# Block-diagonal probability tiles in the token stage of a memory-augmented attention kernel, one core

## The chip, the cores and the metric

The kernel runs on one core of a Trainium2 chip. The metric is the device time of one execution in microseconds (us). The core has a matrix engine (PE, with its weight loads shown apart as PEld), a vector engine (DVE), a scalar engine (ACT), a general engine (POOL) and a queue engine (SP). They run side by side, each in the order of its own instructions, and wait for each other by semaphores. SBUF is the working memory of 128 partitions, PSUM the memory that PE writes to.

## What is computed

The program computes a gated sum of two attention layers, and the gradients of all its inputs. Only the second layer, B, matters here: 2048 tokens in 64 segments of 32, 32 heads of width 128, and 8 memory rows that each segment hands to the next.

```python
for s in range(n_seg):                       # 64 segments of 32 tokens
    h = concatenate([mem, xs], axis=1)       # 8 memory rows, 32 tokens
    q, k, v = h @ Wq, h @ Wk, h @ Wv         # per head
    scores = where(mask, q @ k.T * scale, -1e9)
    p = softmax(scores)
    o = p @ v
    o = o @ Wo
    mem = o[:M]
    outs.append(o[M:])
...
_out, _vjp = jax.vjp(_f, ...)
_grads = _vjp(grad_out)
```

Token rows attend to the 32 tokens of their own segment and to the 8 memory rows of their segment. Backward, with dP the gradient of the probabilities and dS = P * (dP - row sum) * scale, the gradient of q is dS times the keys. Both products, P times the values and dS times the keys, have a part over the 32 tokens and a part over the memory rows.

## The kernel before

The memory rows of all segments are run first, in a chain over the segments. The token rows no longer depend on each other after that, and one stage (`b_bulk`) does their forward and their backward pass. A later stage, woven with a second chain, does the backward pass of the memory rows.

`b_bulk` works on groups: 128 tokens (four segments) by four heads, 128 groups in all. Four groups make a chunk, for which inputs are loaded and outputs stored on SP's queue. The main loop runs over ticks `t`. In each tick the list `order` names 18 steps, and a step with the number `n` works on group `t - n`, so that a tick holds a step of some ten different groups. The order of the steps is the order of the instructions on every engine; nothing is rearranged by a scheduler in this stage.

The names in a tick, in the order of the list:

- `st_QT` transposes q of group t on PE into the PSUM buffer `x_tr` (two such buffers serve all transpositions in turn). `dS` of group t-8 rides along as a fifth block. DVE copies the four blocks to `x_qT` (L836), the fifth into the right half of `x_DT` (L822), and transposes the token part of `dS` in 32 by 32 blocks straight from SBUF into its left half (L823).
- `st_KT` does the same with k of group t (`x_kT`) and with `P` of group t-3 (`x_PT`).
- `st_Om` (group t-4) multiplies the memory part: the transposed memory half of `x_PT` times the values of the memory rows, which lie block-diagonally in `x_vmB`, into `x_po`.
- `st_OT` (t-5) transposes o, ACT copies it to `x_oT` (L935), and POOL multiplies it with `x_dOT` into `x_prod` (L938), from which the row sums come. `st_VT` transposes v, copied by ACT. `st_B` (four pieces spread over the tick) multiplies o by Wo into `x_b`.
- `st_SDm` and `st_SDx` compute scores and dP in one PSUM bank, `x_SD`: memory part, then token part. ACT takes the exponential into `x_E` (L891), DVE forms `x_dS` (L897).
- `st_GT` transposes dO; DVE copies it to `x_dOT` (L836).
- `st_Qm` (t-9) is the memory part of dq, into a second `x_po`. `st_K` multiplies for the gradients of the memory's k and v, in every second tick.
- `st_R` (t-2): DVE sums the rows of `x_E` (`x_l`, L911), takes the reciprocal (`x_r`, L913), and POOL multiplies both to `x_P` (L915).
- `st_M` (t-1) masks `x_E` on DVE (L904).
- `st_Ox` (t-4) and `st_Qx` (t-9) add the token parts. For each head i and each segment c a product of 32 by 32 weights with 32 by 128 values, placed on the diagonal of the PE array, sixteen in each step:

```python
self.mm(po[r32, i, :], lhsT=PT[r32, 32 * i:32 * i + 32], rhs=v[r32, i, :],
        start=False, stop=True, tp=(32 * c, 32 * c))
```

ACT copies the result out (L808) into `x_o` or `x_dq`.

DVE's order in a tick is thus: x_qT, x_DT (copy, transposition), x_kT, x_PT (copy, transposition), x_dOT, x_l, x_r, x_dS, mask. POOL's is x_prod, x_P.

Of the kernel before, what the change touches and what calls it, by code (L numbers as in the profile page):

```python
# [10 lines left out]
ALU = mybir.AluOpType  # L11
AX = mybir.AxisListType
BF16 = mybir.dt.bfloat16
# [3 lines left out]
P = 128  # L17
# [8 lines left out]
SEG = 32  # L26
# [25 lines left out]
class Kern:  # L52
# [675 lines left out]
    def b_bulk(self, wp, lp, sp, psum):  # L728
        nc = self.nc
        NTT = self.NTT  # L730
        mx = self.maskX
        mB = {w: [wp.tile([P, 4, 4, E], BF16, name=f"x_{w}mB{i}") for i in range(2)] for w in ("k", "v")}
        mT = {}
        C = {}
        NG = NTT * 8
        NC = NTT * 2

        def load(c, names):
            if c >= NC:
                return  # L740
            tt, h0 = c // 2, 16 * (c % 2)
            d = C.setdefault(c, {})
            for w in names:
                if w == "mT":
                    if c % 2 == 0:
                        mT[tt] = {}
                        for x in ("k", "v"):
                            mT[tt][x] = lp.tile([P, 4, HB, 8], BF16, name=f"x_{x}mT", bufs=2)
                            nc.sync.dma_start(mT[tt][x][:], self.mTd[x][4 * tt:4 * tt + 4].rearrange("s p h t -> p s h t"))
                elif w in ("kB", "vB"):  # L750
                    for i in range(4):
                        nc.sync.dma_start(
                            mB[w[0]][c % 2][32 * i:32 * i + 32, :, i, :],
                            self.mtok[w[0]][tt * 32:(tt + 1) * 32, h0 * P:h0 * P + 2048]
                            .rearrange("r (g i e) -> r g i e", i=4, e=E)[:, :, i, :])
                else:
                    d[w] = lp.tile([P, 16, P], BF16, name=f"x_{w}", bufs=BQ if w in deep else 3)
                    nc.sync.dma_start(d[w][:].rearrange("p h e -> p (h e)"),
                                      self.xtok[w][tt * P:(tt + 1) * P, h0 * P:h0 * P + 2048])
# [5 lines left out]
        def chunk(t, w, shape, bufs):  # L765
            d = C[t // 4]
            if w not in d:
                d[w] = sp.tile(shape, BF16, name=f"x_{w}", bufs=bufs)
            return d[w]

        def view(t):
            return t // 8, t % 8, slice(4 * (t % 4), 4 * (t % 4) + 4), C[t // 4]
# [13 lines left out]
        def flush(end=False):  # L786
            for dst, src in due.pop(0):
                (nc.scalar if end else nc.sync).dma_start(dst, src)
            due.append([])

        def transp(d, r, nm, pt):
            self.tr(pt[:, 4, :], d[:, 1, r, :].rearrange("p i t -> p (i t)"), P)
            o = sp.tile([P, 256], BF16, name=nm, bufs=2)
            return o, d[:, 0, r, :].rearrange("p i t -> p (i t)")

        def attend_m(PT, m):
            po = psum.tile([P, 4, P], F32, name="x_po", bufs=2)
            self.mm(po[:].rearrange("p i e -> p (i e)"), lhsT=PT[:, 128:256], rhs=m.rearrange("p i e -> p (i e)"),
                    start=True, stop=False)
            return po  # L800

        def attend_x(o, po, PT, v):
            for i in range(4):
                for c in range(4):
                    r32 = slice(32 * c, 32 * c + 32)
                    self.mm(po[r32, i, :], lhsT=PT[r32, 32 * i:32 * i + 32], rhs=v[r32, i, :],
                            start=False, stop=True, tp=(32 * c, 32 * c))
            nc.scalar.copy(o, po[:])  # L808

        sc = {}  # L810

        def trans(t, w, nb, ride=None):
            pt = psum.tile([P, 5, P], BF16, name="x_tr", bufs=2)
            if 0 <= t < NG:
                tt, g, r, d = view(t)
                for i in range(4):
                    self.tr(pt[:, i, :], d[w][:, 4 * (g % 4) + i, :], P)
            o2 = ride and ride(pt)
            if 0 <= t < NG:
                trans_out(t, w, nb, pt)  # L820
            if o2:
                nc.vector.tensor_copy(o2[0][:, 128:256], pt[:, 4, :])  # L822
                nc.vector.transpose(o2[0][:, 0:128], o2[1])  # L823

        def trans_out(t, w, nb, pt):
            tt, g, r, d = view(t)
            if w == "v":
                o = chunk(t, "vT", [P, 4, 16, SEG], 2)
                nc.scalar.copy(o[:, :, r, :].rearrange("p s h t -> p h s t"),
                               pt[:, 0:4, :].rearrange("p h (s t) -> p h s t", t=SEG))  # L830
                if t % 4 == 3:
                    for c in range(4):
                        due[1].append((self.vT_dram[4 * tt + c][:, 16 * (t // 4 % 2):16 * (t // 4 % 2) + 16, :], o[:, c]))
                return
            o = sp.tile([P, 4, P], BF16, name=f"x_{w}T", bufs=nb)
            nc.vector.tensor_copy(o[:], pt[:, 0:4, :])  # L836
            sc[w + "T", t] = o

        def ride(t, nm, out):
            def put(pt):  # L840
                if 0 <= t < NG:
                    tt, g, r, d = view(t)
                    o2 = transp(d[nm], r, "x_" + out, pt)
                    sc[out, t] = o2[0]
                    return o2
            return put

        st_QT = lambda t: trans(t, "q", 2, ride(t - 8, "dS", "DT"))
        st_KT = lambda t: trans(t, "k", 2, ride(t - 3, "P", "PT"))
        st_GT = lambda t: trans(t, "dO", 7)  # L850
        st_VT = lambda t: trans(t, "v", 2)

# [65 lines left out]

        def st_Om(t):
            tt, g, r, d = view(t)  # L920
            sc["po", t] = attend_m(sc["PT", t], mB["v"][t // 4 % 2][:, g % 4])

        def st_Ox(t):
            tt, g, r, d = view(t)
            o = chunk(t, "o", [P, 16, P], 2)
            attend_x(o[:, r, :], sc.pop(("po", t)), sc.pop(("PT", t)), d["v"][:, r, :])
            store(t, self.xtok["o"], o)
# [29 lines left out]

        def st_Qm(t):
            tt, g, r, d = view(t)
            sc["pq", t] = attend_m(sc["DT", t], mB["k"][t // 4 % 2][:, g % 4])  # L960

        def st_Qx(t):
            tt, g, r, d = view(t)
            dq = chunk(t, "dq", [P, 16, P], 2)
            attend_x(dq[:, r, :], sc.pop(("pq", t)), sc.pop(("DT", t)), d["k"][:, r, :])
            store(t, self.xtok["dq"], dq)
            if t % 4 == 3:
                C.pop(t // 4)

        def st_K(t):  # L970
# [12 lines left out]
            if t % 4 == 3:  # L983
                c2 = t // 4 % 2
                for i in range(4):
                    dst = self.dmx_dram[tt * 32:(tt + 1) * 32].rearrange("m (g i) w e -> i m g (w e)", i=4)
                    due[1].append((dst[i][:, 4 * c2:4 * c2 + 4, :], dm[32 * i:32 * i + 32].rearrange("p g w e -> p g (w e)")))

        B_ = lambda i: lambda t: st_B(t, i)
        order = [(None, st_QT), (7, B_(0)), (None, st_KT), (7, B_(1)), (4, st_Om), (5, st_OT), (7, B_(2)), (5, st_VT),  # L990
                 (7, B_(3)), (None, st_SDm), (0, st_GT), (9, st_Qm), (2, st_R), (7, st_K),
                 (None, st_SDx), (1, st_M), (4, st_Ox), (9, st_Qx)]
        done = {st_Ox: (4,), st_VT: (5,), st_SDx: (6,), st_K: (7,), st_Qx: (9,)}
        load(0, deep + ("mT", "v"))
        load(1, deep)
        for t in range(NG + 9):
            for n, st in order:
                if n is None:
                    st(t)
                elif 0 <= t - n < NG:  # L1000
                    st(t - n)
                for n in done.get(st, ()):
                    if t - n >= 0 and (t - n) % 4 == 3:
                        c = (t - n) // 4
                        for w in after[n]:
                            load(c + (BQ if w in deep else 3 if w in ("mT", "v") else 2), (w,))
            if t < 2:
                for w in ("v", "k"):
                    nc.vector.memset(mB[w][t][:], 0.0)
                load(t, ("vB", "kB"))  # L1010
                if t == 0:
                    load(1, ("v",))
                    load(2, deep + ("mT", "v"))
                else:
                    for c in range(3, BQ):
                        load(c, deep)
            if t % 4 == 2 and t // 4 - 2 in range(NTT // 4):
                self.dl_rows(t // 4 - 2, sp, psum)
            flush(t > NG)
# [1363 lines left out]
```

## Time and profile before

| | |
|---|---|
| three runs | 5270.73 us median, 5256.26 to 5274.28 |
| profiled execution | 5275.43 us |
| its span | 5273.7 us |
| token stage, 2045 to 2690 us of the span | PE busy 568.0, DVE 401.0, ACT 366.1, POOL 241.9 of 645 us |
| granted PE clock in the span | 0.988 of full speed |

How to read the lines that follow. A row of the timeline has the start in us, the duration in us, the engine, the line of the program, the operation, what it writes and reads (names without buffer numbers), its size, how many were merged into the row (x16), and in brackets the idle time of its engine before it and what ended it. A row of a window has the stretch, its length and the busy time of PE, PEld, DVE, ACT and POOL with the number of instructions, then granted clock, DMA share and GB/s. A row of the waits has the engine and line that waited, the one that it waited for, us in total, how many times, and the longest. A row of groups has busy time and mean ns of one after the bar. A row of a line's or a tile's instructions has min/median/max in ns and the first and last start. L87 and L92 are helpers through which all products and all transpositions of PE are issued.

### The profile page before, as it was taken

The numbers are of one execution on the slowest core, as the hardware profiler recorded it, in microseconds if no ns is written. First come the engines' busy times: TensorE is split into PE (matmuls) and PEld (weight loads), VectorE is DVE, ScalarE is ACT, GpSimd is POOL, SyncE is SP. The second block draws the span as 40 slices with busy tenths as digits, with TensorE's granted clock in tenths as the row PEclk, the third lists the DMA queues.
The fourth block names the chain that finished last, engine by engine and source line by source line (L and its number), as shares of the span: only waits on it lengthen the run. The fifth ranks groups of instructions, "written<-read, shape, count | busy, mean of one in ns | idle before, by whom it ended". The sixth has DMA issues, their size and how long they took to land. (4 is left out here: it accounts for less than half of the span.)

```text
span 5273.7 us, 216258 instructions
## 1 busy us (share of the span) xinstructions
PE 5025.2 (95%) x92973; PEld 2779.6 (53%) x93152; DVE 3526.8 (67%) x7041; ACT 3272.5 (62%) x4701; POOL 2166.9 (41%) x4164
## 2 busy tenths in 40 slices
PE   8999999999999998988889999999999999999999
PEld 5444444444444445666655555555555577754445
DVE  4348888888888887666657778788888841333332
ACT  4237888888888886555557777777777732222211
POOL 3015666665655655333323444444444421111213
PEclk9999999999999999999999999999999999999999
DMA  8855676656765456888885788878888787965654
GB/s 273 266 149 133 140 137 143 138 138 138 144 137 127 116 111 176 260 258 253 241 282 159 175 183 181 177 179 180 181 182 177 169 198 213 267 217 187 189 165 138
DMA packets 1070902, 959.23 MB, mean 182 GB/s; under 512 B 618245, under 2 KB 926413, under 8 KB 1059956
## 3 DMA queue, kind: packets, MB, share of 16 engines
q1 hardware_dynamic: 958556, 695.16, 54.7%
q0 software_dynamic: 102032, 240.46, 15.1%
q8 instruction: 728, 11.93, 1.0%
q10 hardware_dynamic: 9352, 9.77, 0.6%
q14 instruction: 234, 1.92, 0.1%
HBM read 518.26 MB, written 375.52 MB: 169 GB/s over the span
## 5 line engine op out<-in xcount | busy, mean ns | idle before, releaser
L2098 DVE TENSOR_TENSOR b_dS<-b_dP,b_E 128x512 bf16<-128x512 f32 x2048 | 1317.5, 685 | 559.9 <-PE b_dP L87 253.6
L1933 DVE TENSOR_TENSOR a_W<-a_dP,a_E 128x512 bf16<-128x512 f32 x2048 | 1313.8, 683 | 227.9 <-issue 103.6
L2047 ACT ACTIVATE b_E<-b_S 128x1024 bf16<-128x1024 f32 x1024 | 1049.2, 1025 | 608.5 <-PE b_dP L87 491.0
L1902 ACT ACTIVATE a_E<-a_S 128x1024 bf16<-128x1024 f32 x1024 | 1050.0, 1025 | 244.5 <-PE a_dP L87 163.6
L87 PE MATMUL a_acc<-a_E,l_VK 128*32 128x512 bf16 x4096 | 594.5, 385 | 7.8 <-issue 2.8
L87 PE MATMUL r_pj<-WT,r_dT 128*32 128x288 bf16 x12288 | 489.3, 290 | 8.9 <-issue 4.6
L87 PE MATMUL w_acc<-w_d,w_h 128*128 128x512 bf16 (+1 forms) x2342 | 480.0, 380 | 3.7 <-issue 1.1
L87 PEld LDWEIGHTS <-b_QS 32*128 32x128 bf16 (+1 forms) x8192 | 238.6, 91 | 439.9 <-issue 394.1
L87 PE MATMUL b_S<-b_KV,b_QS 32*128 32x512 bf16 x2048 | 404.7, 386 | 36.1 <-ACT b_E L2047 21.2
L87 PE MATMUL a_S<-a_QD,l_KV 32*128 32x512 bf16 x2048 | 398.7, 383 | 40.7 <-ACT a_E L1902 39.1
L87 PE MATMUL b_dP<-b_KV,b_QS 32*128 32x512 bf16 x2048 | 404.0, 389 | 3.1 <-DVE b_dS L2098 1.7
L87 PE MATMUL a_acc<-a_W,l_WK 128*32 128x512 bf16 x2048 | 405.5, 390 | 0.3 <-DVE a_W L1933 0.2
L87 PE MATMUL b_acc<-b_dS,b_QS 128*18 128x512 bf16 x2048 | 398.7, 384 | 1.8 <-issue 1.2
L87 PE MATMUL b_acc<-b_E,b_QS 128*18 128x512 bf16 x2048 | 397.6, 384 | 0.8 <-issue 0.8
L87 PE MATMUL a_dP<-a_QD,l_KV 32*128 32x512 bf16 x2048 | 398.2, 385 | 0.0
L87 PEld LDWEIGHTS <-hm 128*32 128x32 bf16 x7680 | 263.8, 96 | 196.8 <-issue 15.0
L87 PEld LDWEIGHTS <-r_dT 128*32 128x32 bf16 x12288 | 277.1, 96 | 135.5 <-issue 87.2
L87 PEld LDWEIGHTS <-w_h 128*128 128x128 bf16 (+1 forms) x2528 | 214.5, 100 | 245.2 <-issue 17.7
L938 POOL TENSOR_TENSOR x_prod<-x_dOT,x_oT 128x512 bf16<-128x512 bf16 x128 | 148.0, 1156 | 299.5 <-ACT x_oT L935 282.5
L87 PEld LDWEIGHTS <-l_KV 32*128 32x128 bf16 x4096 | 123.8, 91 | 250.5 <-issue 210.1
L87 PEld LDWEIGHTS <-l_WK 128*32 128x32 bf16 x2048 | 98.9, 93 | 218.7 <-issue 218.7
L87 PE MATMUL x_b<-WoN,x_oT 128*128 128x288 bf16 x1024 | 211.0, 290 | 1.2 <-issue 1.2
(475 smaller groups left out, 10114.0 us busy)
## 6 DMA issues: line engine op xcount, KB each, us to landing
b_QS<-qs_dram SPq DMA_DIRECT2D x233, 200.0 KB
dOx_dram<-p_tok SPq DMA_DIRECT2D x16, 1024.0 KB
c_vx<-vx_dram SPq DMA_DIRECT2D x64, 256.0 KB
krow_dram<-c_k POOLq DMA_DIRECT2D x64, 256.0 KB
qrow_dram<-c_q POOLq DMA_DIRECT2D x64, 256.0 KB
vrow_dram<-c_v POOLq DMA_DIRECT2D x64, 256.0 KB
x_q<-qx_dram SPq DMA_DIRECT2D x32, 512.0 KB
x_dO<-dOx_dram SPq DMA_DIRECT2D x32, 512.0 KB
```

The source lines that it names most:

```text
L87: return self.nc.tensor.matmul(out, lhsT, rhs, start=start, stop=stop, tile_position=tp, skip_group_check=True)
L938: nc.gpsimd.tensor_tensor(out=sc["prod", t][:], in0=sc["dOT", t][:], in1=oT[:], op=ALU.mult)
L1902: nc.scalar.activation(E_[n][:], S.pop(n)[:], ACT.Exp, scale=SCALEA)
L1933: nc.vector.tensor_tensor(out=W_[n][:, i, :], in0=dP[i][:], in1=E_[n][:, i, :], op=ALU.mult)
L2047: nc.scalar.activation(E_[n][:], S.pop(n)[:], ACT.Exp, scale=SCALEA)
L2098: nc.vector.tensor_tensor(out=D_[n][:, i, :], in0=dP[i][:], in1=E_[n][:, i, :], op=ALU.mult)
```

## The change

The 32 by 32 blocks are spread into tiles that hold a full 128 by 128 block-diagonal matrix for each of four heads, zero outside the diagonal. One full-height product per head then does the work of four small ones.

- For the probabilities there are two fixed tiles, `x_PTd`, zeroed once before the loop. After the transposition of `P`, DVE copies each of its four partition groups of 32 into its place on the diagonal: four copies a tick.
- For the gradients POOL multiplies the transposed `dS`, repeated four times, by the block mask `bmask`, into a fresh tile `x_DTd` of 128 by 512: one operation a tick. It is issued in `st_QT`, before `x_prod` and `x_P` of the same tick.
- The riding fifth block is no longer copied by itself. One copy moves all five blocks, 640 columns, into `x_qT` or `x_kT`, and the memory product takes its weights from the fifth.

```diff
+        diag = [wp.tile([P, 4, 4, SEG], BF16, name=f"x_PTd{i}") for i in range(2)]
...
-        def transp(d, r, nm, pt):
+        def transp(d, r, pt):
             self.tr(pt[:, 4, :], d[:, 1, r, :].rearrange("p i t -> p (i t)"), P)
-            o = sp.tile([P, 256], BF16, name=nm, bufs=2)
-            return o, d[:, 0, r, :].rearrange("p i t -> p (i t)")
+
+        def block_diag(d, r, t, nm):
+            o = sp.tile([P, 4, SEG], BF16, name=f"x_{nm}", bufs=2)
+            nc.vector.transpose(o[:].rearrange("p i q -> p (i q)"), d[:, 0, r, :].rearrange("p i t -> p (i t)"))
+            if nm == "PT":
+                full = diag[t % 2]
+                for c in range(4):
+                    r32 = slice(32 * c, 32 * c + 32)
+                    nc.vector.tensor_copy(full[r32, :, c, :], o[r32])
+            else:
+                full = sp.tile([P, 4, 4, SEG], BF16, name="x_DTd", bufs=2)
+                nc.gpsimd.tensor_tensor(out=full[:], in0=o[:].unsqueeze(2).to_broadcast([P, 4, 4, SEG]), op=ALU.mult,
+                                        in1=self.bmask[:, :, 0:1].unsqueeze(1).to_broadcast([P, 4, 4, SEG]))
+            sc[nm, t] = full
...
         def attend_x(o, po, PT, v):
             for i in range(4):
-                for c in range(4):
-                    r32 = slice(32 * c, 32 * c + 32)
-                    self.mm(po[r32, i, :], lhsT=PT[r32, 32 * i:32 * i + 32], rhs=v[r32, i, :],
-                            start=False, stop=True, tp=(32 * c, 32 * c))
+                self.mm(po[:, i, :], lhsT=PT[:, i].rearrange("p c q -> p (c q)"), rhs=v[:, i, :], start=False, stop=True)
             nc.scalar.copy(o, po[:])
...
-            if o2:
-                nc.vector.tensor_copy(o2[0][:, 128:256], pt[:, 4, :])
-                nc.vector.transpose(o2[0][:, 0:128], o2[1])
...
-            o = sp.tile([P, 4, P], BF16, name=f"x_{w}T", bufs=nb)
-            nc.vector.tensor_copy(o[:], pt[:, 0:4, :])
-            sc[w + "T", t] = o
+            lo, hi = 0 if 0 <= t < NG else 4, 5 if rode else 4
+            if lo < hi:
+                o = sp.tile([P, 4 if w == "dO" else 5, P], BF16, name=f"x_{w}T", bufs=nb)
+                nc.vector.tensor_copy(o[:, lo:hi, :], pt[:, lo:hi, :])
+                if lo == 0:
+                    sc[w + "T", t] = o
+                if rode:
+                    rode(o[:, 4, :])
...
-            sc["po", t] = attend_m(sc["PT", t], mB["v"][t // 4 % 2][:, g % 4])
+            sc["po", t] = attend_m(sc.pop(("PTm", t)), mB["v"][t // 4 % 2][:, g % 4])
...
+        for x in diag:
+            nc.vector.memset(x[:], 0.0)
         for t in range(NG + 9):
```

More of the change, by code (lines that the diff above doesn't have):

```diff
@@ L789, in flush @@
             due.append([])
-        def transp(d, r, nm, pt):
+        def transp(d, r, pt):
             self.tr(pt[:, 4, :], d[:, 1, r, :].rearrange("p i t -> p (i t)"), P)
-            o = sp.tile([P, 256], BF16, name=nm, bufs=2)
-            return o, d[:, 0, r, :].rearrange("p i t -> p (i t)")
+        def block_diag(d, r, t, nm):
[11 more added lines that the diff above has]
+            sc[nm, t] = full
         def attend_m(PT, m):
             po = psum.tile([P, 4, P], F32, name="x_po", bufs=2)
-            self.mm(po[:].rearrange("p i e -> p (i e)"), lhsT=PT[:, 128:256], rhs=m.rearrange("p i e -> p (i e)"),
+            self.mm(po[:].rearrange("p i e -> p (i e)"), lhsT=PT, rhs=m.rearrange("p i e -> p (i e)"),
                     start=True, stop=False)
@@ L817, in trans, with trans_out @@
                     self.tr(pt[:, i, :], d[w][:, 4 * (g % 4) + i, :], P)
-            o2 = ride and ride(pt)
-            if 0 <= t < NG:
-                trans_out(t, w, nb, pt)
-            if o2:
[L822 to L826, printed above, removed]
+            trans_out(t, w, nb, pt, ride and ride(pt))
+        def trans_out(t, w, nb, pt, rode):
             if w == "v":
+                tt, g, r, d = view(t)
                 o = chunk(t, "vT", [P, 4, 16, SEG], 2)
@@ L842, in put @@
                     tt, g, r, d = view(t)
-                    o2 = transp(d[nm], r, "x_" + out, pt)
-                    sc[out, t] = o2[0]
-                    return o2
+                    transp(d[nm], r, pt)
+                    return lambda o: (sc.update({(out + "m", t): o}), block_diag(d[nm], r, t, out))
             return put
@@ L959, in st_Qm @@
             tt, g, r, d = view(t)
-            sc["pq", t] = attend_m(sc["DT", t], mB["k"][t // 4 % 2][:, g % 4])
+            sc["pq", t] = attend_m(sc.pop(("DTm", t)), mB["k"][t // 4 % 2][:, g % 4])
         def st_Qx(t):
```

## The prediction

> **What bounds the kernel now.** I read the page first. Its chain of waits covers only the last fifth of the span, so it says nothing of the token stage, and that stage has to be read from its own stretch.
>
> ```profile
> span 5273.7 us, 216258 instructions
> PE 5025.2 (95%) x92973; PEld 2779.6 (53%) x93152; DVE 3526.8 (67%) x7041; ACT 3272.5 (62%) x4701; POOL 2166.9 (41%) x4164
> ```
>
> The profiled execution took 5275.4 us, 1.7 us more than its span and 4.7 us more than the median of the three runs (5270.7). The windows view gives the stage's row, and the view of the tile x_po gives its ticks.
>
> ```profile
> 2045.00:2690.00 645.00, 567.96 (x14826) 426.35 (x14920) 400.99 (x1450) 366.08 (x728) 241.93 (x286) 0.96 0.83 251
> ```
>
> ```profile
> L808 ACT CAST x_o<-x_po x128: 580/580/618, 2061.5 to 2663.5; 128x512 bf16<-128x512 f32 x128
> ```
>
> PE (first pair) is busy 88% of 645 us, DVE (third) 62%, POOL (fifth) 38%. From the first to the last x_o copy are 127 ticks: (2663.5 - 2061.5) / 127 = **4.74 us a tick**. No other stage shares the time, so what a tick gains or loses goes straight into the span. The waits of PE's weight loads and of PE, between 2100 and 2600 us (some 105 ticks):
>
> ```profile
> PEld L92 <- DVE x_PT L822: 28.6, 94, 0.3
> PEld L92 <- DVE x_DT L822: 27.1, 87, 0.5
> ```
>
> ```profile
> PE x_po L87 <- issue: 13.4, 10, 2.8
> PE x_SD L87 <- issue: 12.2, 11, 2.6
> PE x_m L87 <- issue: 8.9, 6, 2.6
> ```
>
> So PE is not alone the bound. In nearly nine ticks of ten its weight loads wait twice, 0.30 us each (28.6 / 94, 27.1 / 87), until DVE has emptied a transposition buffer; and 27 times it stands for lack of instructions, 34.5 us in all, 0.33 us a tick. What DVE does in a tick is in the timeline, DVE alone, then POOL:
>
> ```profile
> 2300.04 0.41 DVE L911 TENSOR_REDUCE x_l<-x_E 128x4 f32<-128x256 bf16 x1
> 2300.48 0.18 DVE L913 RECIPROCAL x_r<-x_l 128x4 f32<-128x4 f32 x1
> 2300.79 0.42 DVE L897 SCALAR_TENSOR_TENSOR x_dS<-x_SD,x_P 128x256 bf16<-128x256 f32 x1
> 2301.13 0.37 DVE L904 TENSOR_TENSOR x_E<-x_E,maskX 128x128 uint32<-128x128 uint32 x1
> 2301.42 0.41 DVE L836 COPY x_qT<-x_tr 128x512 bf16<-128x512 bf16 x1
> 2301.75 0.21 DVE L822 COPY x_DT<-x_tr 128x128 bf16<-128x128 bf16 x1
> 2301.89 0.29 DVE L823 STREAM_TRANSPOSE x_DT<-x_dS 128x128 bf16<-128x128 bf16 x1
> 2302.11 0.38 DVE L836 COPY x_kT<-x_tr 128x512 bf16<-128x512 bf16 x1
> 2302.42 0.20 DVE L822 COPY x_PT<-x_tr 128x128 bf16<-128x128 bf16 x1
> 2302.55 0.28 DVE L823 STREAM_TRANSPOSE x_PT<-x_P 128x128 bf16<-128x128 bf16 x1
> 2303.90 0.42 DVE L836 COPY x_dOT<-x_tr 128x512 bf16<-128x512 bf16 x1 [1.06 <-PE x_tr L92]
> 2304.24 0.41 DVE L911 TENSOR_REDUCE x_l<-x_E 128x4 f32<-128x256 bf16 x1
> ```
>
> ```profile
> 2300.74 0.61 POOL L915 TENSOR_TENSOR x_P<-x_E,x_r 128x256 bf16<-128x256 bf16 x1 [0.38 <-DVE x_r L913]
> 2303.23 1.16 POOL L938 TENSOR_TENSOR x_prod<-x_dOT,x_oT 128x512 bf16<-128x512 bf16 x1 [1.88 <-ACT x_oT L935]
> 2304.94 0.61 POOL L915 TENSOR_TENSOR x_P<-x_E,x_r 128x256 bf16<-128x256 bf16 x1 [0.55 <-DVE x_r L913]
> ```
>
> From one x_l to the next are 4.20 us: a tick without a stall. DVE is idle once, 1.06 us before x_dOT. POOL is idle until x_oT comes.
>
> **A row that decides.** The mask (L904) reads two SBUF tensors. Above it begins while POOL makes x_P, which ends at 2300.74 + 0.61 = 2301.35, and it ends 0.15 us later.
>
> ```profile
> L904 DVE TENSOR_TENSOR x_E<-x_E,maskX x128: 279/368/610, 2051.5 to 2653.7; 128x128 uint32<-128x128 uint32 x128
> ```
>
> ```profile
> 72.34 0.30 POOL L1846 COPY xtail<-gotok 128x128 bf16<-128x128 bf16 x1
> 72.38 0.43 DVE L1739 TENSOR_SCALAR gotok<-gotok,omg_all 128x576 bf16<-128x576 bf16 x1
> ```
>
> ```profile
> 72.59 0.37 POOL L1846 COPY xtail<-gotok 128x128 bf16<-128x128 bf16 x1
> ```
>
> ```profile
> L1739 DVE TENSOR_SCALAR gotok<-gotok,omg_all x16: 358/364/465, 62.9 to 85.1; 128x576 bf16<-128x576 bf16 x16
> ```
>
> ```profile
> L1846 POOL COPY xtail<-gotok x15: 293/309/373, 63.7 to 86.6; 128x128 bf16<-128x128 bf16 x15
> ```
>
> Alone the mask takes 0.28 us; beside x_P 0.37, since it waits for x_P's end. The preparation shows the same for a DVE operation with one tensor, SBUF to SBUF: 0.43 us in place of 0.36, ending 0.17 us after the POOL copy; and the next POOL copy, begun meanwhile, is stretched from 0.31 to 0.37. DVE and POOL exclude each other here. Copies out of PSUM and x_l do not show it: the x_l at 2304.24 takes its usual 0.41 us although x_prod still runs until 2304.39. The Trainium skill, "SBUF — State Buffer" (SBUF: two separate sides), states such an exclusive lock of a port pair for the whole instruction; the two pairs of rows agree.
>
> **The change part by part.**
>
> *Products.* Per tick 32 small products and their weight loads become 8 and 8. The time they stream does not change: PE alone shows
>
> ```profile
> 2300.11 0.40 PE L87 MATMUL x_po<-x_v,x_PT 32*32 32x128 bf16 x16
> 2300.34 0.39 PE L87 MATMUL x_po<-x_k,x_DT 32*32 32x128 bf16 x16
> 2300.67 0.40 PE L92 MATMUL x_tr<-identB,x_q 128*128 128x128 bf16 x4
> ```
>
> that sixteen 32x32 products take 0.40 us from the first start to the last end, and four full-height products of the same 128 columns (the x_q transpositions) 0.40 us too. From start to start, though, the first sixteen take 0.23 us and the second 0.33, so some 0.10 us for the change of tile shape goes away. This lies beside DVE's work, for which PE waits anyway, by more than 0.10 us each time; it is worth nothing unless DVE gets faster, and 0.10 us without that cover. Forty-eight PE instructions fewer, of about 219 a tick (14826 + 14920 in 645 us), cut the 0.33 us of missing instructions by a fifth if the stalls go with the count: -0.07 us.
>
> *Merged copies on DVE.* The 128-column copies of L822 go, and those of L836 grow to 640 columns. Rows of that width and of the other prices:
>
> ```profile
> L82 DVE COPY xT<-trx 128x640 bf16<-128x640 bf16 x8 | 3.7, 482 | 3.2 <-PE trx L92 3.2
> ...
> L361 DVE COPY c_PBm<-seln 128x256 bf16<-128x256 bf16 x1 | 0.2, 163 | 0.0
> ```
>
> ```profile
> L281 POOL TENSOR_TENSOR r_dSB<-r_dS,bmask 128x512 bf16<-128x512 bf16 x64 | 69.3, 1083 | 0.7 <-DVE r_dS L1221 0.7
> ```
>
> 0.48 us against 0.41, +0.07 each; from start to start 0.33 + 0.07 = 0.40 in place of 0.33 + 0.14. Both buffers come free 0.06 to 0.1 us sooner.
>
> *Diagonal tile of the gradients, on POOL.* One 128x512 product a tick: 1.08 us (r_dSB, same mask) to 1.16 us (x_prod). In POOL's order it stands ahead of x_prod and x_P. Its load, 1.1 + 1.16 + 0.61 = 2.9 us a tick, is no bound. It starts when x_DT's transposition is done: 0.40 + 0.29 after x_qT's start, plus 0.08 (x_r's end, 2300.66, to x_P) = 0.78; it ends at 1.86 to 1.94. Before, x_prod could start 2303.23 - 2301.42 = 1.81 after x_qT, so now it follows at once and POOL is occupied from 0.78 to about 3.1.
>
> *Diagonal tile of the probabilities, on DVE.* Four copies, 32 partitions by 128 columns, SBUF to SBUF. No row has this shape. Below: 0.13 us (start to start of the 128-column x_PT copy, 2302.42 to 2302.55); above: 0.16 us (256 columns, c_PBm). I take 0.15, 0.6 us for four. They would fit into the 1.06 us that DVE waits for PE's x_dO, and cost nothing there; without that cover they cost 0.6 us. But they are asked for at 0.40 + 0.22 + 0.38 + 0.28 and a hand-over of 0.06 = 1.34 after x_qT, in the middle of the new POOL product, and one-tensor SBUF operations like L1739 wait for POOL. By the Trainium skill, "VectorE: DVE Perf Modes" (What auto-detection actually checks), a 16-bit copy inside SBUF with even outer dimensions uses both read ports; no run here shows it for this shape.
>
> I take that they wait. The first copy slips in at POOL's change of instruction, as L1739 did; x_prod takes the port next, stretched by 0.06 us, until 3.08 to 3.16; the other three follow at 0.15 each, and x_dOT starts at 3.5 to 3.65 after x_qT, not 2.48. Queued behind it on DVE are x_l, x_r, and with them POOL's x_P, then x_dS and the mask: 0.34 + 1.38 to the next x_qT, unchanged, since the mask already waits for x_P. The tick becomes 5.2 to 5.4 us; I take **5.25**. It hides PE's savings, and all but the longest instruction stalls, for which I leave 0.05: 5.30.
>
> *Rest.* Two tiles are zeroed once. No DMA is issued or moved on any queue; the few that POOL issues in the stage stand behind 1.1 us more, and nothing waits on them. Buffers for the new tiles turn over every second tick.
>
> **Sum.** Both diagonal tiles are made in ticks 8 to 130, 123 of them: 123 x (5.30 - 4.74) = +69 us on 5275.4, 5344 us; against the median 5340 us. Its own range is 5310 (a second copy slips in too, tick 5.05, stalls hidden) to 5360 (tick 5.40).
>
> **The rivals.**
>
> *No waiting (faster).* If the small copies don't exclude POOL, they end at 1.34 + 0.6 = 1.94, before PE gives x_dO at 2.48. x_P on POOL is ready as before, for x_prod ends at 3.1 and x_r at 3.4. The tick loses up to 0.10 (buffers freed sooner, shape change) and 0.07 (stalls), worth 123 x 0.17 = 21 us: 5250 us. For it: x_l and the mask's neighbours that read PSUM ignore POOL, and no row has 32 partitions. Against: the row of L1739.
>
> *All four copies pass in the gap (same).* Then x_prod waits until about 2.5 and ends near 3.65; x_P starts there instead of at 3.52 (x_dOT at 2.48, then 0.34, 0.44, 0.18 and 0.08), and the mask ends 0.15 after x_P, at 4.41 in place of 4.28. A tick costs 0.13 where it was shortest, less 0.07 to 0.1: 5270 us, give or take 12. For it: L1739 did get in ahead of a POOL instruction that had begun. Against: that was one instruction, and here DVE lets go of the port three times while POOL is waiting.
>
> *Everything waits (slower still).* x_prod takes the port ahead of the first copy, and all four follow at 0.2 us each, a little above c_PBm: x_dOT at 3.16 + 0.8 = 3.96, tick 5.68; less the stalls, which all vanish in it, 123 x (5.68 - 4.74) = +116, 5387 us; at 0.15 us a copy 5360. I put this case at 5375. What would speak for it is a POOL that asks for the port as early as it begins (72.59, before the 72.64 at which its last one ends); the DVE row that got in speaks against it.
>
> **How the numbers follow.** Chances: forecast 0.60, slower still 0.11, pass in the gap 0.11, no waiting 0.18. The predicted time is 5340. A difference under 0.3% (16 us) cannot be told from none. Range 5262 to 5385: it leaves out most of the no-waiting case, takes in the passing one and both ends of the waiting ones; the forecast's own stands above. Faster 0.18 (no waiting, and a little of the passing case, less its own part within 16 us), same 0.10, slower 0.72.
>
> **What would show it.** POOL's new product at 1.08 to 1.16 us; the copies to x_PTd with a mean far above 0.15 us, the later ones ending just after x_prod's end; DVE's wait for PE before x_dOT gone; x_o ticks 5.25 us apart; PE's wait for x_tr buffers larger. I am wrong if the copies all take about 0.15 us while POOL runs, or if the tick stays under 4.9 us.

## The result and the profile after

The changed kernel takes 5339.4 us in the median of four runs (5338.0 to 5345.8), against 5268.2 us for the kernel before, measured beside it (four runs). The ratio is 1.0146, with a 95% interval of 1.0128 to 1.0164: 1.5% slower. The profiled execution took 5345.8 us.

The page, the stage's window (PE, PEld, DVE, ACT, POOL, busy us and instructions) and the row of x_o that gives the tick:

```profile
span 5344.0 us, 210816 instructions
...
PE 5036.8 (94%) x90080; PEld 2791.6 (52%) x90080; DVE 3811.3 (71%) x7310; ACT 3267.8 (61%) x4701; POOL 2305.0 (43%) x4292
```

```profile
2045.00:2690.00 645.00, 517.56 (x10745) 395.59 (x10742) 621.97 (x1561) 319.40 (x652) 334.98 (x371) 0.98 0.72 225
```

```profile
L818 ACT CAST x_o<-x_po x128: 579/580/603, 2059.3 to 2744.5; 128x512 bf16<-128x512 f32 x128
```

A tick has grown from 4.74 to (2744.5 - 2059.3) / 127 = 5.40 us. DVE counts as busy for 96% of the stage, PE for 80%. But busy is not working here. DVE's timeline of one tick, in three pieces so that the copies stand apart:

```profile
2310.56 0.48 DVE L843 COPY x_qT<-x_tr 128x640 bf16<-128x640 bf16 x1
2310.97 0.29 DVE L797 STREAM_TRANSPOSE x_DT<-x_dS 128x128 bf16<-128x128 bf16 x1
2311.19 0.45 DVE L843 COPY x_kT<-x_tr 128x640 bf16<-128x640 bf16 x1
2311.57 0.28 DVE L797 STREAM_TRANSPOSE x_PT<-x_P 128x128 bf16<-128x128 bf16 x1
2311.88 0.66 DVE L802 COPY x_PTd<-x_PT 32x128 bf16<-32x128 bf16 x1
...
2312.56 1.10 DVE L802 COPY x_PTd<-x_PT 32x128 bf16<-32x128 bf16 x1
...
2313.68 0.39 DVE L802 COPY x_PTd<-x_PT 32x128 bf16<-32x128 bf16 x2
2314.10 0.43 DVE L843 COPY x_dOT<-x_tr 128x512 bf16<-128x512 bf16 x1
2314.55 0.42 DVE L920 TENSOR_REDUCE x_l<-x_E 128x4 f32<-128x256 bf16 x1
2315.01 0.18 DVE L922 RECIPROCAL x_r<-x_l 128x4 f32<-128x4 f32 x1
2315.10 0.39 DVE L906 SCALAR_TENSOR_TENSOR x_dS<-x_SD,x_P 128x256 bf16<-128x256 f32 x1
2315.41 0.61 DVE L913 TENSOR_TENSOR x_E<-x_E,maskX 128x128 uint32<-128x128 uint32 x1
2315.95 0.48 DVE L843 COPY x_qT<-x_tr 128x640 bf16<-128x640 bf16 x1
```

POOL in the same tick:

```profile
2311.43 1.07 POOL L805 TENSOR_TENSOR x_DTd<-x_DT,bmask 128x512 bf16<-128x512 bf16 x1 [0.94 <-DVE x_DT L797]
2312.46 1.16 POOL L947 TENSOR_TENSOR x_prod<-x_dOT,x_oT 128x512 bf16<-128x512 bf16 x1
2315.26 0.61 POOL L924 TENSOR_TENSOR x_P<-x_E,x_r 128x256 bf16<-128x256 bf16 x1 [1.65 <-DVE x_r L922]
```

Read the ends (start plus duration). x_DTd ends at 2312.50, the first copy at 2312.54. x_prod ends at 2313.62, the second copy at 2313.66. The last two, with POOL idle, take 0.39 us together. Four equal instructions took 0.66, 1.10, 0.19 and 0.19 us, and what lies between is POOL. The group of all copies between 2100 and 2600 us has a mean of 0.54 us:

```profile
L802 DVE COPY x_PTd<-x_PT 32x128 bf16<-32x128 bf16 x365 | 197.3, 541 | 7.0
```

The tick shown is the rule: in 117 of the 128 groups of four, the first two copies are long (over 0.3 us) and the last two are not. Of all 512 copies 242 are long, and all but one of these end 0.04 to 0.06 us after one of POOL's two products, 119 after x_DTd and 122 after x_prod. PE's waits between 2100 and 2600 us, where there were waits for DVE's copies and for instructions (the first two of four rows):

```profile
PE x_tr L92 <- POOL x_P L924: 79.1, 87, 1.0
PE x_tr L92 <- DVE x_dOT L843: 8.5, 14, 0.7
```

PE now waits 0.9 us (79.1 / 87) in nearly every tick for x_P, the end of the chain copies, x_dOT, x_l, x_r, x_P. No wait of PE for instructions is left in its list; its weight loads (PEld) still have such waits, 63.9 us (38.0 + 25.9) where they had 71.3.

The 127 ticks from the first x_o to the last take 685.2 us instead of 602.0, 83 us more; the whole span is 70 us longer. From the last x_o to the end of the span were 2610 us before and are 2600 now, and the first x_o comes 2 us earlier. In the experiments below this rest varies between 2599 and 2620 us, and I have not traced where.

### The profile page after: what moved, and what is told of

It is laid out like the page before. It is cut to its first block, busy times and chain, and to the rows that moved or that the text cites. A ratio compares the mean times of both kernels' runs of the same rounds, so it can differ in the third digit from the quotient of the medians.

```text
span 5344.0 us, 210816 instructions
## 1 busy us (share of the span) xinstructions
PE 5036.8 (94%) x90080; PEld 2791.6 (52%) x90080; DVE 3811.3 (71%) x7310; ACT 3267.8 (61%) x4701; POOL 2305.0 (43%) x4292
## 5 line engine op out<-in xcount | busy, mean ns | idle before, releaser
L802 DVE COPY x_PTd<-x_PT 32x128 bf16<-32x128 bf16 x512 | 269.3, 526 | 9.7
L944 ACT COPY x_oT<-x_tr 128x512 bf16<-128x512 bf16 x128 | 75.0, 586 | 241.1 <-PE x_tr L92 237.6
```

Of the source, the lines that this page charges most:

```text
L802: nc.vector.tensor_copy(full[r32, :, c, :], o[r32])
L944: nc.scalar.copy(oT[:], pt[:, 0:4, :])
```

## The experiments

Eight kernels were run. e1 and e2 leave out one of the two suspected operations each and keep the other; e3 moves one, e4 and e5 replace the copies, and e6 to e8 look at what is left. The ratios are to the kernel before, measured beside each on the same chip: e1 to e4 on one (before: 5273.9 us), e5 to e8 on another (before: 5272.6 us). So ratios can be compared across the table, and times less well. A tick is worked out from the first and last x_o as above, from the one profiled execution; those of e4 and e7 took 13 and 17 us more than their medians.

| | time, us | ratio (95%) | tick, us | waits of a copy, us |
|---|---|---|---|---|
| the change | 5339.4 | 1.0146 (1.0128 to 1.0164) | 5.40 | 0.66 and 1.10 |
| e1, no copies | 5247.8 | 0.9951 (0.9935 to 0.9967) | 4.58 | |
| e2, no POOL product | 5284.7 | 1.0014 (0.9999 to 1.0030) | 4.84 | 1.05 |
| e3, POOL product moved | 5284.8 | 1.0021 (1.0006 to 1.0036) | 4.85 | 1.06 |
| e4, transpositions in place of copies | 5254.4 | 0.9960 (0.9942 to 0.9979) | 4.61 | none |
| e5, copies on ACT | 5378.6 | 1.0194 (1.0167 to 1.0221) | 5.59 | none |
| e6, e4 with small products | 5275.9 | 1.0002 (0.9986 to 1.0019) | 4.78 | none |
| e7, e4 with five buffers for k | 5251.5 | 0.9953 (0.9936 to 0.9969) | 4.59 | none |
| e8, before with five buffers for k | 5281.5 | 1.0011 (0.9996 to 1.0026) | 4.71 | |

### e1: without the copies

```diff
-                for c in range(4):
-                    r32 = slice(32 * c, 32 * c + 32)
-                    nc.vector.tensor_copy(full[r32, :, c, :], o[r32])
```

> The four diagonal copies of the probabilities on DVE are left out, so the token part of o is computed with zeros; POOL's product x_DTd stays where it is, ahead of x_prod. Theory (the copies wait for POOL's two products, and hold up DVE's queue): without them DVE is idle before x_dOT again, the tick returns to 4.2 to 4.5 us and the time to 5235 to 5275 us. Rival 1 (POOL's longer order delays x_prod and x_P): nothing changes, 5330 to 5345. Rival 2 (DVE has 0.6 us more to do a tick): also 5235 to 5275.

5247.8 us. POOL does all that it does in the changed kernel, in the same order, and the loss is gone: POOL's longer order by itself costs nothing. Rival 1 falls. Rival 2 is not touched yet. DVE waits for PE before x_dOT again, as it did before (105.2 us, 90 times, between 2100 and 2600 us):

```profile
DVE x_dOT L840 <- PE x_tr L92: 108.7, 96, 2.9
```

The tick, 4.58 us, is above the 4.2 to 4.5 expected.

### e2: without POOL's product

```diff
+        zd = [wp.tile([P, 4, 4, SEG], BF16, name=f"x_DTz{i}") for i in range(2)]
...
-                full = sp.tile([P, 4, 4, SEG], BF16, name="x_DTd", bufs=2)
-                nc.gpsimd.tensor_tensor(out=full[:], in0=o[:].unsqueeze(2).to_broadcast([P, 4, 4, SEG]), op=ALU.mult,
-                                        in1=self.bmask[:, :, 0:1].unsqueeze(1).to_broadcast([P, 4, 4, SEG]))
+                full = zd[t % 2]
...
-        for x in diag:
+        for x in diag + zd:
```

> POOL's product x_DTd is left out (two fixed zero tiles in its place, so the token part of dq is zero); the four copies on DVE stay. Theory (copies wait for POOL): the first copies are asked for before x_prod starts, so at most one of them waits for x_prod; copies of 0.13 to 0.19 us, 5240 to 5290 us. Rival 1 (POOL's order): 5235 to 5275. Rival 2 (0.6 us more DVE work a tick bounds the stage): stays at 5320 to 5345.

5284.7 us: the same copies, and by the ratios (1.0014 against 1.0146) nine tenths of the loss gone. So it is not DVE's own work either (rival 2). The row of the copies shows what is left, min, median and max in ns:

```profile
L803 DVE COPY x_PTd<-x_PT x512: 182/185/1062, 2059.1 to 2673.6; 32x128 bf16<-32x128 bf16 x171
```

The median copy takes 0.19 us, but one of four, the last, still meets x_prod and takes 1.05 us (in 116 of the 128 groups).

### e3: POOL's product behind x_P

```diff
-                full = sp.tile([P, 4, 4, SEG], BF16, name="x_DTd", bufs=2)
...
-            sc[nm, t] = full
+                later.append((t, o))
+                return
...
+        def st_D(tick):
+            for t, o in later:
+                full = sp.tile([P, 4, 4, SEG], BF16, name="x_DTd", bufs=2)
+                nc.gpsimd.tensor_tensor(...)
+                sc["DT", t] = full
+            later.clear()
...
-                 (7, B_(3)), (None, st_SDm), (0, st_GT), (9, st_Qm), (2, st_R), (7, st_K),
+                 (7, B_(3)), (None, st_SDm), (0, st_GT), (9, st_Qm), (2, st_R), (None, st_D), (7, st_K),
```

> The same work, moved: POOL's product x_DTd is issued behind x_P at the end of the tick instead of ahead of x_prod. Theory: it then runs from x_P's end to about 1.0 us after x_qT's start, before the copies are asked for at 1.34; the copies take 0.2 us each, tick 4.2 to 4.5, 5235 to 5280 us, possibly below the kernel before since PE loses the change of shape and part of its missing instructions. Rival 1 (POOL's total work is too much): 5330 to 5345. Rival 2 (DVE's work): 5320 to 5345.

5284.8 us, 5 us above the range. No work is left out here; only the time at which POOL works is another. DVE's copies and POOL in one tick of e3:

```profile
2312.00 0.58 DVE L802 COPY x_PTd<-x_PT 32x128 bf16<-32x128 bf16 x3
...
2312.59 1.06 DVE L802 COPY x_PTd<-x_PT 32x128 bf16<-32x128 bf16 x1
```

```profile
2310.57 1.11 POOL L813 TENSOR_TENSOR x_DTd<-x_DT,bmask 128x512 bf16<-128x512 bf16 x1
2312.41 1.18 POOL L956 TENSOR_TENSOR x_prod<-x_dOT,x_oT 128x512 bf16<-128x512 bf16 x1 [0.73 <-ACT x_oT L953]
```

x_DTd is over at 2311.68, before the copies are asked for, as the theory has it, and three copies pass in 0.58 us. The fourth comes 0.18 us after x_prod has begun and ends 0.06 us after it. I had taken the copies to be through before x_prod; they miss it by one. One long copy of 1.06 us in place of two of 0.66 and 1.10 us makes the tick 0.55 us shorter (5.40 to 4.85) and, by the ratios (1.0146 to 1.0021), gives back 66 us.

### e4: transpositions straight into the diagonal tile

```diff
-            o = sp.tile([P, 4, SEG], BF16, name=f"x_{nm}", bufs=2)
-            nc.vector.transpose(o[:].rearrange("p i q -> p (i q)"), d[:, 0, r, :].rearrange("p i t -> p (i t)"))
+            src = d[:, 0, r, :].rearrange("p i t -> p (i t)")
             if nm == "PT":
                 full = diag[t % 2]
                 for c in range(4):
                     r32 = slice(32 * c, 32 * c + 32)
-                    nc.vector.tensor_copy(full[r32, :, c, :], o[r32])
+                    nc.vector.transpose(full[r32, :, c, :], src[r32].rearrange("p (i t) -> p i t", t=SEG))
             else:
+                o = sp.tile([P, 4, SEG], BF16, name=f"x_{nm}", bufs=2)
+                nc.vector.transpose(o[:].rearrange("p i q -> p (i q)"), src)
```

> The transposition of P writes its four partition groups straight into the diagonal tile (four small transpositions in place of one and four copies); POOL's product stays ahead of x_prod. Transpositions did not wait for POOL in the kernel before. Theory (an exclusive port for copies): each takes 0.2 to 0.25 us however POOL runs, done by 2.0 us after x_qT, tick 4.2 to 4.5, 5230 to 5275 us. Rival 1 (POOL's order delays x_prod and x_P): 5330 to 5345. Rival 2 (DVE's work a tick): 5320 to 5345, as four transpositions cost about what the copies cost alone.

5254.4 us, faster than both kernels: 0.4% under the one before (0.9960, 0.9942 to 0.9979). POOL's product stands where the change put it, and DVE writes the same tile from four partition groups at the same place of its order. The row of the transpositions, and DVE and POOL in one tick of e4:

```profile
L801 DVE STREAM_TRANSPOSE x_PTd<-x_P x512: 277/302/309, 2054.9 to 2640.9; 32x128 bf16<-32x128 bf16 x171
```

```profile
2315.98 1.23 DVE L801 STREAM_TRANSPOSE x_PTd<-x_P 32x128 bf16<-32x128 bf16 x4
2317.31 0.42 DVE L844 COPY x_dOT<-x_tr 128x512 bf16<-128x512 bf16 x1
2317.77 0.42 DVE L921 TENSOR_REDUCE x_l<-x_E 128x4 f32<-128x256 bf16 x1
```

```profile
2315.85 1.07 POOL L806 TENSOR_TENSOR x_DTd<-x_DT,bmask 128x512 bf16<-128x512 bf16 x1 [1.13 <-DVE x_DT L804]
2316.88 1.15 POOL L948 TENSOR_TENSOR x_prod<-x_dOT,x_oT 128x512 bf16<-128x512 bf16 x1
```

512 transpositions lie between 0.28 and 0.31 us, under POOL's products as elsewhere. 435 of them run wholly under an operation of POOL. A transposition does not wait for POOL where a copy into the same tile does; why it does not, no run shows. That four of 0.30 us are more work than one of 0.28 and four copies of 0.19 refutes rival 2 a second time. A transposition takes 0.30 us, not the 0.2 to 0.25 expected, and the tick 4.61 us, not 4.2 to 4.5; the time is inside its range.

### e5: the copies on ACT

```diff
-                    nc.vector.tensor_copy(full[r32, :, c, :], o[r32])
+                    nc.scalar.copy(full[r32, :, c, :], o[r32])
```

> The kernel as changed, but the four copies of the probabilities into the diagonal tile run on ACT instead of DVE; POOL's product stays ahead of x_prod. Theory (only DVE and POOL exclude each other): the copies on ACT take their own time whatever POOL does, and the long waits go; ACT gets about 1.2 us more a tick and has the room (319 of 645 us busy), 5250 to 5300 us. Rival (any copy from SBUF to SBUF beside POOL waits, whatever its engine): the copies show 0.6 and 1.1 us, 5320 us or more.

The copies' row is as the theory has it, the time is not: 5378.6 us, the slowest of all.

```profile
L802 ACT COPY x_PTd<-x_PT x512: 293/296/298, 2051.3 to 2761.9; 32x128 bf16<-32x128 bf16 x171
```

```profile
2311.52 1.25 ACT L802 COPY x_PTd<-x_PT 32x128 bf16<-32x128 bf16 x4 [1.09 <-DVE x_PT L797]
2312.79 0.58 ACT L944 COPY x_oT<-x_tr 128x512 bf16<-128x512 bf16 x1
```

```profile
PE x_tr L92 <- ACT x_oT L944: 106.8, 88, 1.5
```

No copy takes more than 0.30 us, and 129 of the 512 run wholly under an operation of POOL: ACT's copies and POOL do not exclude each other. But the four stand in ACT's order ahead of the copy to x_oT, after 1.09 us in which ACT waits for DVE's transposition. x_oT and the PSUM buffer that it empties come late, and PE waits for them 106.8 us, 88 times, between 2100 and 2600 us. I had counted ACT's share of busy time, and not what is queued behind the copies.

### e6: e4 with small products

```diff
-                self.mm(po[:, i, :], lhsT=PT[:, i].rearrange("p c q -> p (c q)"), rhs=v[:, i, :], start=False, stop=True)
+                for c in range(4):
+                    r32 = slice(32 * c, 32 * c + 32)
+                    self.mm(po[r32, i, :], lhsT=PT[r32, i, c], rhs=v[r32, i, :], start=False, stop=True, tp=(32 * c, 32 * c))
```

> Experiment e4 (small transpositions straight into the diagonal tile), but the products are again sixteen of 32 by 32 a step, taken from the blocks of the diagonal tiles. It adds 48 PE instructions a tick and nothing else. Theory (full-height products are worth the instruction stalls and the change of shape): the waits for instructions come back, 0.2 to 0.4 us a tick, 5275 to 5305 us. Rival (PE's side is hidden behind DVE, so the products are worth nothing): as e4, 5245 to 5262.

5275.9 us, where e4 has 5254.4; the intervals of the two ratios do not overlap, nor does that of e7, which is e4 with one more buffer and was measured beside e6. The part of the change that was its point, the full-height products, is worth 0.4%, shape and missing instructions together. PE's waits in e6 and in e4, from their lists:

```profile
PE x_po L87 <- issue: 13.8, 10, 3.2
PE x_SD L87 <- issue: 13.0, 12, 3.1
PE x_tr L92 <- issue: 7.0, 5, 2.8
PE x_b L87 <- issue: 4.1, 4, 2.6
```

```profile
PE x_tr L92 <- DMA x_k<-kx_dram: 23.0, 10, 5.4
...
PE x_po L87 <- issue: 2.3, 2, 1.5
```

With 48 PE instructions more a tick the waits for instructions are there, 37.9 us in these four rows; without them 2.3 us in the largest, and 4.1 in all rows of this kind.

### e7 and e8: five buffers for k

e4's first row above is new: PE waits 23.0 us for loads of k. In e7 and in e8 the chunks of k get a fifth buffer.

```diff
-                    d[w] = lp.tile([P, 16, P], BF16, name=f"x_{w}", bufs=BQ if w in deep else 3)
+                    d[w] = lp.tile([P, 16, P], BF16, name=f"x_{w}", bufs=5 if w == "k" else BQ if w in deep else 3)
...
-                            load(c + (BQ if w in deep else 3 if w in ("mT", "v") else 2), (w,))
+                            load(c + (5 if w == "k" else BQ if w in deep else 3 if w in ("mT", "v") else 2), (w,))
...
+                    load(BQ, ("k",))
```

> Experiment e4 with five buffers in place of four for the chunks of k, loaded one chunk earlier. e4 shows PE waiting some 30 us for loads of x_k. Theory (with the waits on DVE gone the late loads of k bound e4): these waits go and the time falls to 5220 to 5240. Rival (the load is late because the DMA engines are full, and an earlier issue only moves the wait to another load): 5245 to 5260.

> The kernel before with five buffers for the chunks of k: the control of the experiment with five buffers. Before shows no wait for x_k, so no change: 5262 to 5282 us. If it gains as much as e7 gains over e4, the fifth buffer is a matter of its own.

e7 takes 5251.5 us, not to be told from e4 and in the rival's range, not the theory's; e8 is not to be told from before. The wait for k has gone in e7, and another stands in its place:

```profile
PE x_po L87 <- ACT x_o L819: 10.3, 8, 2.3
```

and ACT's copies to x_o wait 17.1 us, ten times, for stores of o. That the DMA engines (busy share 0.86 in e7 between 2045 and 2690 us, 0.83 before) now bound the stage was only argued; what the two runs show is that one more buffer does not help.

## Why the prediction was right

5340 us were predicted, 5339.4 measured. Most of this agreement is mechanism, some of it is luck.

*The waits.* The step that decided, that the copies wait for POOL's products, is shown: by the ends in the profile, by e1 and e2 (either of the two alone loses little or nothing), by e3 (the same work at another time), and by e4 (the same place, another operation). Its details also came out: the first copy slips in between the two products, and x_prod goes ahead of the second. One did not: x_prod is not stretched by 0.06 us, its mean is 1.155 us where it was 1.156. The stated range, 5262 to 5385, says less than these rows: it takes in three of the four cases. Counted from x_qT's start, the copies were asked for at 1.32 (predicted 1.34), x_prod ended at 3.06 (3.08 to 3.16), and x_dOT started at 3.54 (3.5 to 3.65).

*The copy.* 0.19 us against 0.15, above the bound of 0.16 that I had taken from a copy of twice the columns.

*The way back to x_qT.* I had taken 1.72 us from x_dOT as unchanged; it is 1.85. x_l starts 0.45 us after x_dOT instead of 0.34. So the tick became 5.39 and not 5.25.

*The stalls for instructions.* I left 0.05 us a tick; none remain in PE's list. Tick 5.40 in all against 5.30, and 83 us in the stage against 69. That the time agrees to a microsecond is luck: what follows the last x_o got 11 us shorter (2610.2 to 2599.5) and the first x_o came 2 us earlier, which no step of mine had.

*The savings.* The change of tile shape is gone: between the start of the second group of products and that of x_q lie 0.22 us, not 0.33.

```profile
2313.55 0.39 PE L87 MATMUL x_po<-x_k,x_DTd 128*128 128x128 bf16 x4
2313.77 0.39 PE L92 MATMUL x_tr<-identB,x_q 128*128 128x128 bf16 x4
```

The estimate for a kernel without the waits, 21 us faster, comes near what e4 and e1 show (0.4% and 0.5% of 5273.9 us, 21 and 26 us), and the 0.17 us a tick that e6 loses against e4 (4.78 - 4.61) is just the sum of its two parts, 0.10 for the shape and 0.07 for missing instructions. The second part was mis-sized all the same. The waits for instructions differ by some 0.35 us a tick (40.8 us in 500 in e6, 4.1 in e4): nearly all of before's 0.33 us vanish, not a fifth. But e4 waits 23.0 us for loads of k where e6 waits 3.7, some 0.18 us a tick, and my sum had no such wait. The two errors work against each other.

*The rivals.* No waiting, all copies in the gap, and everything waiting are each excluded by the same four durations, 0.66, 1.10, 0.19 and 0.19 us.

## What to carry to other kernels

An operation that fits into an engine's idle time costs nothing only if nothing else excludes it there: before a copy inside SBUF is put on DVE, see what POOL is doing at that moment, and read the ends of the two, not the busy shares. Where DVE must move data beside a busy POOL, an operation that does not wait for it (here a transposition that writes the final layout) can be longer and still win. When an operation is moved to an idle engine, read what stands behind it in that engine's order before its free time.

## What was not expected

*One group after another.* The copies start only when the one before has ended (the last two take 0.39 us together, about twice the 0.19 us of one), and after them x_l waits for x_dOT's end: x_dOT to x_l is 0.45 us in the changed kernel and 0.46 in e4 (2317.31 to 2317.77), 0.34 in e1, where DVE has no operation on a part of the partitions:

```profile
2313.14 0.43 DVE L840 COPY x_dOT<-x_tr 128x512 bf16<-128x512 bf16 x1 [2.79 <-PE x_tr L92]
2313.48 0.41 DVE L917 TENSOR_REDUCE x_l<-x_E 128x4 f32<-128x256 bf16 x1
```

It is not the idle time ahead of x_dOT: in e4 the median is 0.46 us after a wait as without one. The Trainium skill, "VectorE: DVE Perf Modes" (Two Vector instructions with no wait between them), gives a model for it: an instruction is held until all earlier ones are done when it reads SBUF from another group of 32 partitions than the last one that read SBUF. The last copy reads the fourth group, x_dOT reads PSUM, and x_l the first group; the three runs agree.

*Stalls that end all at once.* A cut of 22% in PE's instructions (some 219 to 171 a tick) took nearly all of PE's own waits for instructions away, 37.5 us before against 4.1 in e4 between 2100 and 2600 us, not 22% of them. The weight loads keep most of theirs (71.3 and 58.5 us), and what ends these waits no run shows.
